# First group of a fused attention and two-layer expert kernel: float64 weights converted in double slabs on ScalarE and VectorE

## The chip, the cores and the metric

The kernel runs as one program on one core of a Trainium2 chip. The metric is the device time of one execution in microseconds; three runs of the kernel before took 1424.27, 1425.4 and 1425.7 us (median 1425.4).

## The reference

Three stages over 4608 tokens of width 512. Attention is within chunks of 64 tokens. The second stage's weights arrive as float64, everything else that is multiplied as float32.

```python
# q, k, v: 8 batches, 8 heads, 576 positions, 64 wide; chunks of 64
scores = scale * np.matmul(q_c, k_c.transpose(0, 1, 2, 4, 3))
attn = softmax(scores)
x = np.matmul(attn, v_c)              # to 4608 x 512, float32
h = x @ w_in                          # 512 x 2048, float64
g = h * (1.0 / (1.0 + np.exp(-h)))
x = (g @ w_out).astype(np.float32)    # 2048 x 512, float64
logits = x @ w_gate + modality_bias[modality_id]
e_idx = np.argmax(logits, axis=1)     # one of 8 experts per token
for e in range(8):                    # w1: 8 x 512 x 1024, w2: 8 x 1024 x 512
    h = np.maximum(x[e_idx == e] @ w1[e], 0.0)
    out[e_idx == e] = gate_w * (h @ w2[e])
```

## The kernel before

The tokens are worked in 18 blocks of 256 (two tiles of 128). A block goes through its attention, the first product with w_in (16 columns f of 128 hidden values), the activation, and the second product with w_out. Every value that enters a product of these two layers is cut in two parts, high and low, so that three products in a faster format stand for one in float32: `hi*x_hi`, `hi*x_lo`, `lo*x_hi` (L452, L483 to L485).

Blocks 0 and 1 form the **first group**: they run together, column by column, while w_in and w_out are still being read and converted. The converted weights then stay on chip (`big1`, `big2`) for the other 16 blocks, which run one at a time. A group has 18 steps: step st does the first product of column st and, two steps later (`LAG`), the second product of column st - 2. In the first group a step has two half steps, one for each block.

A **slab** is 128 columns of w_in or 128 rows of w_out, 512 KB of float64. Its conversion has four parts:

- `load_w64`: a DMA on SP's queue into one of four buffers, issued in the program's order when the slab four places earlier has been converted;
- `conv_p`: ScalarE takes the absolute value of the high words (L381), VectorE a maximum with a constant (L382);
- `conv_a`, all on VectorE: shift and mask (L395), the sign and top bit merged in (L399), the top bits of the low word merged in (L403); the result is float32;
- `conv_b`: ScalarE casts to the high part (L424), GpSimd subtracts to get the low part (L426).

One slab is converted in each half step, two half steps or more ahead of its use. The activation of a column is g = (tanh(h/2) + 1) h: tanh on ScalarE (L459, `th`), the rest on VectorE (L461, `g`). `g_parts` cuts it into `gh` on ScalarE (L467) and `gl`, on GpSimd in the first group (L470) and on VectorE later. The hidden values h stand in PSUM tiles `psh` of one bank each, of which there are two; a block's half step uses half of a bank.

Each engine runs its instructions in the order in which the program writes them; `weave` emits the parts of several generators in turn. Attention of the next block's tiles is spread over the half steps by lists (`att_side`). Before the first group stands the attention of tiles 0 to 3 in eight turns, with short products that nothing reads (`heat`) in between, and with the first slabs' conversion placed by `CONV_TURNS`. The queue of SP carries nearly all loads and stores, in order. When the conversion is done its memory becomes the pool `late`, which holds among others `wgb`, the router's weights, copied to all partitions; `dot` (L505) reads them on VectorE, a few per step (`pump`).

Of the kernel before, what the change touches and what calls it, by code (L numbers as in the profile page):

```python
# [42 lines left out]
def attention_moe_moe_kernel(  # L43
# [71 lines left out]
    def consts():  # L115
# [3 lines left out]
        # triu[r, c] = 1 where r < c  # L119
# [9 lines left out]
        # the tiles in the order of the experts, the lone one left out  # L129
# [224 lines left out]
    raw64 = {}  # L354
    # first layer's slabs, 2 f + (0: w_in, 1: w_out), in the order in which they are needed
    ORD = [0, 2] + [x for f in range(NF - 2) for x in (2 * f + 1, 2 * f + 4)] + [2 * NF - 3, 2 * NF - 1]
    w_in32 = w_in.bitcast(U32).rearrange("(k p) (f w) -> p k f w", p=P, w=2)
    w_out32 = w_out.bitcast(U32).rearrange("(f p) (d w) -> f p d w", p=P, w=2)

    def load_w64(conv, n):  # L360
        if n >= 2 * NF:
            return
        f, i = divmod(ORD[n], 2)
        if i == 0:
            a = conv.tile([P, KD, P, 2], U32, tag="raw", bufs=RAWB, name="ra")
# [976 lines left out]
```

## Time and profile before

| | us |
|---|---|
| runs, median of 3 | 1425.4 (1424.27 to 1425.7) |
| span of the profiled execution | 1423.4 |
| TensorE busy | 1385.9 (97%) |
| VectorE busy | 996.3 (70%) |
| ScalarE busy | 612.3 (43%) |
| GpSimd busy | 236.2 (17%) |

The profile is of one execution. Its span runs from the first to the last instruction; the runs' median is 2.0 us above it. The profiler's names for the engines are PE (TensorE, with PEld for its weight loads), DVE (VectorE), ACT (ScalarE), POOL (GpSimd) and SP (the queue that issues the DMAs). The duration of an instruction on VectorE or ScalarE holds some time in which the next one has already started, so that what a row of instructions costs is read from start to start.

### The profile page before, as it was taken

What the parts mean: (1) busy time and instruction counts of PE and PEld (TensorE: products, weight loads), DVE (VectorE), ACT (ScalarE), POOL (GpSimd) and SP (SyncE); (2) the same over time, 40 slices, a digit from 0 to 9 for tenths busy, and PEclk for the clock granted to TensorE, in tenths of its full rate; (3) what the DMA queues carried; (4) which work ended last, traced back from release to release, by engine and by line L of the source; (5) the groups of instructions that cost most, each with busy time, mean ns of one, the idle gap of its engine ahead of it and who ended that gap; (6) DMA issues with size and microseconds to landing.
All of it is one profiled execution on the core that took longest, in us unless ns stands there. A gap on an engine that the chain in (4) does not pass through costs nothing. (4 is left out here: it accounts for less than half of the span.)

```text
span 1423.4 us, 26828 instructions
## 1 busy us (share of the span) xinstructions
PE 1385.9 (97%) x9819; PEld 1231.9 (87%) x9819; DVE 996.3 (70%) x2430; ACT 612.3 (43%) x1294; POOL 236.2 (17%) x237
## 2 busy tenths in 40 slices
PE   8878999999999999999999999999999999999997
PEld 7767889888888888988888888889889998898996
DVE  6999678667766766766776677675577666666664
ACT  5454333333333333333333333343455555555554
POOL 2665300000000000000000000021322323232311
PEclk9899999999999999999999999999999999999999
DMA  8643413212311321321231132051677766676662
GB/s 202 169 125 116 144 35 61 52 30 40 60 30 32 60 42 20 60 52 29 40 60 29 32 60 38 12 130 39 205 249 217 235 217 222 207 233 212 221 219 85
DMA packets 246747, 153.82 MB, mean 108 GB/s; under 512 B 189730, under 2 KB 197958, under 8 KB 246480
## 3 DMA queue, kind: packets, MB, share of 16 engines
q1 hardware_dynamic: 238352, 133.07, 35.9%
q0 software_dynamic: 8256, 18.96, 3.7%
q8 instruction: 79, 1.29, 0.4%
q14 instruction: 60, 0.49, 0.1%
HBM read 132.48 MB, written 20.01 MB: 107 GB/s over the span
## 5 line engine op out<-in xcount | busy, mean ns | idle before, releaser
L452 PE MATMUL psh<-xh,big 128*128 128x256 f32 x2304 | 465.2, 287 | 18.4 <-DVE g L461 18.2
L452 PEld LDWEIGHTS psh<-xh,big 128*128 128x128 f32 x2304 | 376.0, 191 | 39.2 <-DVE g L461 26.0
L452 PE MATMUL psh<-xl,big 128*128 128x256 f32 x1152 | 326.3, 283 | 0.0
L452 PEld LDWEIGHTS psh<-xl,big 128*128 128x128 f32 x1152 | 219.5, 191 | 7.9 <-DVE xl L351 0.2
L461 DVE SCALAR_TENSOR_TENSOR g<-th,psh 128x256 f32<-128x256 f32 x288 | 120.2, 417 | 139.9 <-ACT th L459 138.9
L483 PE MATMUL psc<-big,gh 128*128 128x512 f32 x544 | 218.0, 401 | 0.0
L914 PE MATMUL psh<-xgh,big 128*128 128x256 f32 x1152 | 217.4, 281 | 0.2 <-DVE big L731 0.2
L485 PE MATMUL psc<-big,gl 128*128 128x512 f32 x544 | 214.7, 395 | 2.1 <-DVE gl L470 2.1
L484 PE MATMUL psc<-big,gh 128*128 128x512 f32 x544 | 215.5, 396 | 0.0
L459 ACT ACTIVATE th<-psh 128x256 f32<-128x256 f32 x288 | 110.3, 383 | 200.1 <-PE psh L452 195.9
L505 DVE CUSTOM_DVE_ANT_0 dump<-x2t,wgb 128x512 bf16<-128x512 f32 x272 | 185.0, 680 | 8.2 <-ACT x2t L494 6.4
L467 ACT CAST gh<-g 128x256 fp32r<-128x256 f32 x288 | 116.8, 405 | 166.4 <-DVE g L461 166.0
L914 PEld LDWEIGHTS psh<-xgh,big 128*128 128x128 f32 x1152 | 181.7, 188 | 3.7 <-DVE big L731 0.5
L602 POOL DMA_INDIRECT perm<-rpg,rdi x36 | 36.9, 1025 | 763.6 <-DVE rdi L601 634.8
L914 PE MATMUL psh<-xgl,big 128*128 128x256 f32 x576 | 161.9, 281 | 0.2 <-DVE xgl L905 0.2
L924 DVE SCALAR_TENSOR_TENSOR hl<-psh,hh 128x256 fp32r<-128x256 f32 x144 | 60.8, 424 | 126.1 <-ACT hh L923 126.1
L923 ACT ACTIVATE hh<-psh 128x256 fp32r<-128x256 f32 x144 | 55.4, 385 | 187.8 <-PE psh L914 185.7
L470 DVE TENSOR_TENSOR gl<-g,gh 128x256 fp32r<-128x256 f32 x256 | 107.6, 420 | 25.3 <-ACT gh L467 25.3
L485 PEld LDWEIGHTS psc<-big,gl 128*128 128x128 f32 x544 | 102.4, 188 | 26.2 <-DVE gl L470 2.6
L483 PEld LDWEIGHTS psc<-big,gh 128*128 128x128 f32 x544 | 103.0, 189 | 16.2 <-issue 2.7
L484 PEld LDWEIGHTS psc<-big,gh 128*128 128x128 f32 x544 | 102.6, 189 | 13.3
L914 PEld LDWEIGHTS psh<-xgl,big 128*128 128x128 f32 x576 | 108.8, 189 | 3.8 <-DVE xgl L905 0.5
(237 smaller groups left out, 2073.7 us busy)
## 6 DMA issues: line engine op xcount, KB each, us to landing
rb<-in_moe_w_dram SPq DMA_DIRECT2D x144, 256.0 KB
wr<-in_moe_w_dram SPq DMA_DIRECT2D x68, 512.0 KB
x2d<-x2t SPq DMA_DIRECT2D x36, 256.0 KB
ra<-in_moe_w_in_dram SPq DMA_DIRECT2D x16, 512.0 KB
rb<-in_moe_w_out_dram SPq DMA_DIRECT2D x16, 512.0 KB
qk<-in_q_dram SPq DMA_DIRECT2D x240, 32.0 KB
qk<-in_k_dram SPq DMA_DIRECT2D x240, 32.0 KB
vn<-in_v_dram SPq DMA_DIRECT2D x28, 256.0 KB
```

Source lines behind the costliest of these rows:

```text
L452: nc.tensor.matmul(hps[:, :256], lhsT=w, rhs=x[:, kk, :], start=n == 0, stop=n == 3 * KD - 1)
L459: nc.scalar.activation(out=th, in_=hps[:, :256], func=ACTF.Tanh, scale=0.5)
L461: nc.vector.scalar_tensor_tensor(out=g, in0=th, scalar=1.0, in1=hps[:, :256], op0=ALU.add, op1=ALU.mult)
L467: nc.scalar.copy(gh, g)
L470: eng.tensor_tensor(out=gl, in0=g, in1=gh.bitcast(F32), op=ALU.subtract)
L483: nc.tensor.matmul(a, lhsT=gh[:, c], rhs=wh, start=f == 0, stop=False)
L484: nc.tensor.matmul(a, lhsT=gh[:, c], rhs=wl, start=False, stop=False)
L485: nc.tensor.matmul(a, lhsT=gl[:, c], rhs=wh, start=False, stop=f == NF - 1)
L505: nc.vector.tensor_tensor_reduce(out=dump, in0=x2[j][t], in1=wg[0][:, e, :], scale=1.0, scalar=0.0, op0=ALU.mult, op1=ALU.add, accum_out=l ...
L914: nc.tensor.matmul(hp[:, :256], lhsT=w[:, part, :], rhs=x[:, :, kk * P:(kk + 1) * P], start=i == 0, stop=i == 3 * KD - 1,)
L923: nc.scalar.activation(out=gh, in_=hp[:, :256], func=ACTF.Relu)
L924: nc.vector.scalar_tensor_tensor(out=gl, in0=hp[:, :256], scalar=0.0, in1=gh.bitcast(F32), op0=ALU.max, op1=ALU.subtract)
```

## The change

Slabs become twice as large: 256 columns of w_in or 256 rows of w_out, 1 MB, 16 in all instead of 32, with two buffers instead of four. One double slab is converted per step. In place of absolute value and maximum ScalarE makes one scaled copy of the high words (times 2^-112); the shift's mask and the merge's mask are other constants, so that only the sign comes from the word itself. The subtraction for the low part goes from GpSimd to VectorE, and so does `gl` in the first group. Both blocks' first products of a column go into the two halves of one PSUM bank, and one tanh, one g, one gh and one gl of 512 serve both (`g_pair`). tanh is written in place of g everywhere, and gh and gl share one kind of buffer (`hid`, 5 of 512). At the start the first double slab is loaded behind tile 0's q and k, the second one between the values of tiles 1 and 2. The pool `late` is opened after the group's last step instead of after the last but one, and the dot products of the router start in the fifth step of the next group. (Comments were taken out as well.)

```diff
-RAWB = 4  # float64 slabs that are on chip at a time
+RAWB = 2
-CONV_TURNS = ((2, 2, 3, 6), (3, 3, 5), (4, 6))
+CONV_TURNS = ((1, 6), (1, 6), (2,))
...
+    DS = [(0, 0)] + [x for i in range(NF // 2 - 1) for x in ((0, i + 1), (1, i))] + [(1, NF // 2 - 1)]
+    w_in64 = w_in.bitcast(U32).rearrange("(k p) (i c) -> i p k c", p=P, c=4 * P)
+    w_out64 = w_out.bitcast(U32).rearrange("(i a p) c -> i p a c", p=P, a=2)
...
-        c = conv.tile([P, 512], U32, tag="cc", bufs=RAWB, name="cc")
-        nc.scalar.activation(out=c.bitcast(F32), in_=r3[:, :, 1].bitcast(F32), func=ACTF.Abs)
+        c = conv.tile([P, 1024], U32, tag="cc", bufs=2, name="cc")
+        nc.scalar.activation(
+            out=c.bitcast(F32), in_=raw64[n][:, :, 1].bitcast(F32), func=ACTF.Copy, scale=2.0 ** -112
+        )
...
+        x, r = c64.pop(n), raw64.pop(n)
         nc.vector.tensor_scalar(
-            out=c.bitcast(F32), in0=c.bitcast(F32), scalar1=2.0 ** -15, scalar2=None, op0=ALU.max
-        )
...
-            out=x, in0=c, scalar1=3, scalar2=0x3FFFFFF8, op0=ALU.logical_shift_left, op1=ALU.bitwise_and
+            out=x, in0=x, scalar1=3, scalar2=0x7FFFFFFF, op0=ALU.logical_shift_left, op1=ALU.bitwise_and
         )
         yield
         nc.vector.scalar_tensor_tensor(
-            out=x, in0=hw, scalar=0xC0000000, in1=x, op0=ALU.bitwise_and, op1=ALU.bitwise_or
+            out=x, in0=r[:, :, 1], scalar=0x80000000, in1=x, op0=ALU.bitwise_and, op1=ALU.bitwise_or
         )
         yield
         nc.vector.scalar_tensor_tensor(
-            out=x, in0=lw, scalar=29, in1=x, op0=ALU.logical_shift_right, op1=ALU.bitwise_or
+            out=x, in0=r[:, :, 0], scalar=29, in1=x, op0=ALU.logical_shift_right, op1=ALU.bitwise_or
         )
         y64[n] = x.bitcast(F32)
-        load_w64(conv, n + RAWB)
+        load_w64(n + RAWB)
...
         nc.scalar.copy(hi_o, y)
         yield
-        nc.gpsimd.tensor_tensor(out=lo_o, in0=y, in1=hi_o.bitcast(F32), op=ALU.subtract)
+        nc.vector.tensor_tensor(out=lo_o, in0=y, in1=hi_o.bitcast(F32), op=ALU.subtract)
...
+    def g_pair(f):
+
+        hps = gps.pop((0, f))
+        g = sb.tile([P, 512], F32, tag="g", bufs=3, name="gp")
+        nc.scalar.activation(out=g, in_=hps, func=ACTF.Tanh, scale=0.5)
+        nc.vector.scalar_tensor_tensor(out=g, in0=g, scalar=1.0, in1=hps, op0=ALU.add, op1=ALU.mult)
+        yield
+        gh = hid("gph", [P, 512])
+        nc.scalar.copy(gh, g)
+        yield
+        gl = hid("gpl", [P, 512])
+        nc.vector.tensor_tensor(out=gl, in0=g, in1=gh.bitcast(F32), op=ALU.subtract)
+        for n in range(2):
+            gst[n, f] = (gh[:, n * 256:(n + 1) * 256], gl[:, n * 256:(n + 1) * 256])
...
+        load_w64(0)
         load_nat(1, "qk")
...
-        for names, t in (("qk", 2), (None, 0), (None, 1), ("qk", 3), (None, 2), (None, 3), ("v", 0), ("v", 3),
-                         ("v", 2), ("v", 1)):
-            load_nat(t, names) if names else load_w64(conv, t)
+        for names, t in (("qk", 2), ("qk", 3), ("v", 0), ("v", 1), (None, 1), ("v", 2), ("v", 3)):
+            load_nat(t, names) if names else load_w64(t)
...
                 if first:
+                    hps = ps_h() if st < NF else None
                     for n, j in enumerate(blks):
...
-                        gens += [g_parts(j, st - 1, nc.gpsimd)] if 1 <= st <= NF else []
-                        gens += [once(conv_p, conv, hs + 4), conv_b(hs + 2), conv_a(conv, hs + 3)]
                         if n == 0:
...
+                            gens = [g_pair(st - 1)] if 1 <= st <= NF else []
+                            gens += [fn() for fn in side[2 * st]] + [conv_b(st + 1)]
+                        else:
+                            conv_p(st + 2)
+                            gens = [fn() for fn in side[2 * st + 1]] + [conv_a(st + 2)]
                         weave(gens)
                         if st < NF:
-                            g1_mm(j, st)
+                            g1_mm(j, st, hps[:, n * 256:(n + 1) * 256])
...
-                    gens += pump(2 if last or len(rq) > 16 else 1)
+                    if gi_ > 1 or st >= 4:
+                        gens += pump(2 if last or len(rq) > 16 else 1)
...
-                if first and st == nsteps - 2:
-                    conv_cm.__exit__(None, None, None)
...
             if first:
+                conv_cm.__exit__(None, None, None)
```

Three places in the order of the instructions follow. On VectorE, a half step of the first group before, with a w_out slab (`rb`; `cc` is the slab being converted, `psh` the hidden values):

```order
L461 SCALAR_TENSOR_TENSOR g<-th,psh 128x256
L382 TENSOR_SCALAR cc<-cc 128x512
L395 TENSOR_SCALAR cc<-cc 128x512
L399 SCALAR_TENSOR_TENSOR cc<-rb,cc 128x512
L403 SCALAR_TENSOR_TENSOR cc<-rb,cc 128x512
```

and a step of the first group now (`gp`, `gph` and `gpl` are g, gh and gl of both blocks, `big_70` the converted w_out, `ra` a w_in slab):

```order
L459 SCALAR_TENSOR_TENSOR gp<-gp,psh 128x512
L417 TENSOR_TENSOR big_70<-cc,big_70 128x1024
L465 TENSOR_TENSOR gpl<-gp,gph 128x512
L388 TENSOR_SCALAR cc<-cc 128x1024
L392 SCALAR_TENSOR_TENSOR cc<-ra,cc 128x1024
L396 SCALAR_TENSOR_TENSOR cc<-ra,cc 128x1024
```

Two half steps of five instructions became one step of six: the maximum is gone, the two subtractions L417 and L465 are new, and the rest has twice the elements. On ScalarE, the half step before in which tile 4's transposed q and k are copied (`qT`, `kT`; `big_69` is the converted w_in):

```order
L424 CAST big_69<-cc 128x4x128
L459 ACTIVATE th<-psh 128x256
L231 COPY qT<-psa 128x512
L231 COPY kT<-psa 128x512
L467 CAST gh<-g 128x256
L381 ACTIVATE cc<-rb 128x512
```

and the step now:

```order
L458 ACTIVATE gp<-psh 128x512
L231 COPY qT<-psa 128x512
L231 COPY kT<-psa 128x512
L415 CAST big_70<-cc 128x1024
L462 CAST gph<-gp 128x512
L378 ACTIVATE cc<-ra 128x1024
```

The slab's cast stood ahead of the copies and stands behind them now. On SP, the first DMAs before (`nat` is q, k or v of a tile):

```order
L178 DMA nat<-in_q_dram 128x8x64
L178 DMA nat<-in_k_dram 128x8x64
L178 DMA nat<-in_q_dram 128x8x64
L178 DMA nat<-in_k_dram 128x8x64
L178 DMA nat<-in_q_dram 128x8x64
L178 DMA nat<-in_k_dram 128x8x64
L366 DMA ra<-in_moe_w_in_dram 128x4x256 x2
```

and now:

```order
L178 DMA nat<-in_q_dram 128x8x64
L178 DMA nat<-in_k_dram 128x8x64
L367 DMA ra<-in_moe_w_in_dram 128x4x512
L178 DMA nat<-in_q_dram 128x8x64
L178 DMA nat<-in_k_dram 128x8x64
```

The first slab, which stood behind three tiles' q and k, stands behind those of tile 0.

## Rows read from the trace of the kernel before

**Rows 1.** The page: span, busy time, share and instructions of each engine.

```profile
span 1423.4 us, 26828 instructions
...
PE 1385.9 (97%) x9819; PEld 1231.9 (87%) x9819; DVE 996.3 (70%) x2430; ACT 612.3 (43%) x1294; POOL 236.2 (17%) x237
```

**Rows 2.** Busy time by stretch (us from the start), granted clock, DMA share, GB/s.

```profile
core 0: us, PE busy (x) PEld busy (x) DVE busy (x) ACT busy (x) POOL busy (x), PEclk, DMA share, GB/s
0.00:31.30 31.30, 28.16 (x488) 25.39 (x488) 19.32 (x42) 14.71 (x28) 4.51 (x24) 1.00 0.89 203
31.30:161.80 130.50, 109.53 (x737) 92.36 (x733) 117.02 (x169) 61.95 (x141) 78.44 (x66) 0.93 0.49 141
161.80:971.00 809.20, 806.79 (x5774) 716.86 (x5774) 580.79 (x1677) 298.68 (x698) 41.16 (x40) 1.00 0.24 47
```

**Rows 3.** Waits, 31.3 to 161.8 us: waiter, waited for, total, times, longest.

```profile
PE psh L452 <- DVE g L461: 17.9, 16, 2.2
```

**Rows 4.** Timeline of VectorE: start, duration, line, operation, operands.

```profile
47.72 0.41 DVE L461 SCALAR_TENSOR_TENSOR g<-th,psh 128x256 f32<-128x256 f32 x1
48.05 0.41 DVE L382 TENSOR_SCALAR cc<-cc 128x512 f32<-128x512 f32 x1
48.38 0.41 DVE L395 TENSOR_SCALAR cc<-cc 128x512 uint32<-128x512 uint32 x1
48.83 1.67 DVE L399 SCALAR_TENSOR_TENSOR cc<-ra,cc 128x512 uint32<-128x512 uint32 x1
50.53 1.12 DVE L403 SCALAR_TENSOR_TENSOR cc<-ra,cc 128x512 uint32<-128x512 uint32 x1
51.57 0.41 DVE L461 SCALAR_TENSOR_TENSOR g<-th,psh 128x256 f32<-128x256 f32 x1
```

**Rows 5.** Timeline of GpSimd at the same time.

```profile
48.53 1.42 POOL L426 TENSOR_TENSOR big<-cc,big 128x512 fp32r<-128x512 f32 x1 [1.28 <-ACT big L424]
```

**Rows 6.** Timeline of VectorE in the first attention, GpSimd idle.

```profile
20.07 1.28 DVE L399 SCALAR_TENSOR_TENSOR cc<-ra,cc 128x512 uint32<-128x512 uint32 x2
...
30.11 0.69 DVE L403 SCALAR_TENSOR_TENSOR cc<-rb,cc 128x512 uint32<-128x512 uint32 x1
```

**Rows 7.** Timeline of ScalarE, first attention and first group.

```profile
13.99 1.24 ACT L381 ACTIVATE cc<-ra 128x512 f32<-128x512 f32 x2
...
51.69 0.62 ACT L424 CAST big<-cc 128x512 fp32r<-128x512 f32 x1 [2.09 <-DVE cc L403]
...
52.49 0.58 ACT L231 COPY qT<-psa 128x512 f32<-128x512 f32 x1
...
53.43 0.43 ACT L467 CAST gh<-g 128x256 fp32r<-128x256 f32 x1
```

**Rows 8.** DMA, 80 to 100 us in 40 slices: GB/s moved.

```profile
GB/s 0 0 0 98 311 352 287 16 0 0 0 0 72 141 338 371 127 0 0 0 164 254 328 295 8 0 0 0 135 256 365 289 21 0 0 98 123 221 410 225
```

**Rows 9.** Timeline of TensorE in the first attention: transposes, scores, values of a tile.

```profile
8.90 1.10 PE L227 MATMUL psa<-ident,nat 128*128 128x128 f32 x8
...
10.73 1.15 PE L253 MATMUL psa<-kT,qT 64*64 64x64 f32 x32 [0.50 <-ACT kT L231]
...
26.02 0.97 PE L328 MATMUL psa<-pT,nat 64*64 64x64 f32 x32
```

**Rows 10.** Timeline of VectorE: the last step of tile 3's softmax.

```profile
27.78 0.69 DVE L274 TENSOR_TENSOR p<-p,sm 128x512 f32<-128x512 f32 x1
```

**Rows 11.** Timeline of TensorE at the first group's end, clock up.

```profile
153.24 0.28 PE L452 MATMUL psh<-xh,big 128*128 128x256 f32 x1
...
154.67 0.39 PE L483 MATMUL psa<-big,gh 128*128 128x512 f32 x1
...
156.06 0.40 PE L483 MATMUL psc<-big,gh 128*128 128x512 f32 x1
...
161.42 0.40 PE L485 MATMUL psa<-big,gl 128*128 128x512 f32 x1
```

**Rows 12.** Timeline of SP: issue of a DMA.

```profile
154.41 0.33 SPq L1158 DMA_DIRECT2D wgb<-wgt_d  x1
```

More of the change, by code (lines that the diff above doesn't have):

```diff
@@ L362, in load_w64 @@
+    w_in64 = w_in.bitcast(U32).rearrange("(k p) (i c) -> i p k c", p=P, c=4 * P)
+    w_out64 = w_out.bitcast(U32).rearrange("(i a p) c -> i p a c", p=P, a=2)
+    raw64, c64, y64 = {}, {}, {}
+    def load_w64(n):
+        if n >= NF:
             return
-        f, i = divmod(ORD[n], 2)
-        if i == 0:
-            a = conv.tile([P, KD, P, 2], U32, tag="raw", bufs=RAWB, name="ra")
-            nc.sync.dma_start(out=a, in_=w_in32[:, :, f * P:(f + 1) * P, :])
-        else:
-            a = conv.tile([P, 512, 2], U32, tag="raw", bufs=RAWB, name="rb")
-            nc.sync.dma_start(out=a, in_=w_out32[f])
@@ L387, in conv_a @@
-    def conv_a(conv, n):
-        if n >= 2 * NF:
-            return
-        del raw64[n]
-        c, r3 = c64.pop(n)
-        lw, hw = r3[:, :, 0], r3[:, :, 1]
-        x = c
-        nc.vector.tensor_scalar(
-            out=x, in0=c, scalar1=3, scalar2=0x3FFFFFF8, op0=ALU.logical_shift_left, op1=ALU.bitwise_and
+        which, i = DS[n]
+        if which == 0:
+            a = conv.tile([P, KD, 2 * P, 2], U32, tag="raw", bufs=RAWB, name="ra")
+            nc.sync.dma_start(out=a.rearrange("p k f w -> p k (f w)"), in_=w_in64[i])
+        else:
+            a = conv.tile([P, 2, 512, 2], U32, tag="raw", bufs=RAWB, name="rb")
+            nc.sync.dma_start(out=a.rearrange("p a d w -> p a (d w)"), in_=w_out64[i])
@@ L412, in conv_b @@
             return
[L413 to L414 removed]
         y = y64.pop(n)
[L416 to L418 removed]
+        which, i = DS[n]
+        half, fi = divmod(2 * i, 8)
+        if which == 0:
+            b = big1[:, half * 4:half * 4 + 4, :, fi * P:(fi + 2) * P]
+            hi_o, lo_o = b[:, :, 0], b[:, :, 1]
             y = y.rearrange("p (k f) -> p k f", k=KD)
         else:
[L421 to L423 removed]
+            hi_o, lo_o = big2[:, half * 4 + fi // 2, 0], big2[:, half * 4 + fi // 2, 1]
         nc.scalar.copy(hi_o, y)
         yield
[L426 removed]
+        nc.vector.tensor_tensor(out=lo_o, in0=y, in1=hi_o.bitcast(F32), op=ALU.subtract)
     def weave(gens):
@@ L441, in g1, with g1_mm @@
         g1_act(j, f)
-    def g1_mm(j, f):
+    def g1_mm(j, f, hps=None):
         half, fi = divmod(f, 8)
         hi, lo = xT[j]
-        hps = ps_h()
+        hps = ps_h() if hps is None else hps
         n = 0
@@ L920, in G1 @@
             del xgT[u]
-        gh = sb.tile([P, 256], F32R, tag="gh", bufs=5, name="hh")
-        gl = sb.tile([P, 256], F32R, tag="gl", bufs=5, name="hl")
+        gx = hid("h", [P, 2, 256])
+        gh, gl = gx[:, 0], gx[:, 1]
         nc.scalar.activation(out=gh, in_=hp[:, :256], func=ACTF.Relu)
@@ L996, in attention_moe_moe_kernel @@
         turns = [[] for _ in range(8)]
-        for part, at in zip((lambda n: once(conv_p, conv, n), lambda n: conv_a(conv, n), conv_b), CONV_TURNS):
+        for part, at in zip((lambda n: once(conv_p, n), conv_a, conv_b), CONV_TURNS):
             for n, i in enumerate(at):
@@ L1150, in attention_moe_moe_kernel @@
                     finish_step(j, st)
-                if first and st == nsteps - 2:
-                    conv_cm.__exit__(None, None, None)
-                    late_cm = tc.tile_pool(name="late", bufs=1)
-                    late = late_cm.__enter__()
-                    late_p.append(late)
-                    diag_open()
-                    wgb = late.tile([P, E, DM], F32, name="wgb")
-                    nc.sync.dma_start(
-                        out=wgb.rearrange("p e d -> p (e d)"),
-                        in_=wgt_d.rearrange("(o e) d -> o (e d)", o=1).to_broadcast([P, E * DM]),
-                    )
-                    wg.append(wgb)
-                if not first or st >= NF:
+                if not first:
                     late_gens = pump_late()
             if first:
+                conv_cm.__exit__(None, None, None)
+                late_cm = tc.tile_pool(name="late", bufs=1)
+                late = late_cm.__enter__()
+                late_p.append(late)
+                diag_open()
+                wgb = late.tile([P, E, DM], F32, name="wgb")
+                nc.sync.dma_start(
+                    out=wgb.rearrange("p e d -> p (e d)"),
+                    in_=wgt_d.rearrange("(o e) d -> o (e d)", o=1).to_broadcast([P, E * DM]),
+                )
+                wg.append(wgb)
                 router_bias()
```

61 lines of the change are left out of this document (22 added, 39 removed).

## The prediction

> **What bounds the kernel now.** I read the page's first part, then the busy time by stretch, then the waits of one stretch, then the timelines of single engines there. TensorE is busy in 97% of the span [rows 1], so only a stretch in which it is not can give time back. By stretch, the reader is to see that from 161.8 us on TensorE lacks 2.4 us in 809, while the first group (31.3 to 161.8 us, from its first product to the last of its second products) has it busy for 109.5 of 130.5 us, and at a mean granted clock of 0.93 instead of 1.00; VectorE is busy there for 117.0 us [rows 2]. The waits of that stretch put 17.9 us of TensorE's idle time down to VectorE's g [rows 3]. VectorE's own timeline shows why: a half step is five instructions, back to back, from 47.72 to 51.57, so 3.85 us, of which the two merges of the bits take 1.70 and 1.04 us from start to start [rows 4]. GpSimd works beside them, on its subtraction of one slab (1.42 us) and on gl [rows 5]. The stretch is bound by VectorE; what the change is worth is decided in it and at its two ends.
>
> **What a step costs on VectorE after the change.** First the prices without GpSimd beside. Where GpSimd is idle, two merges of 512 take 1.28 us together and one alone 0.69, so 0.60 from start to start [rows 6]; with g at 256 elements at 0.33 [rows 4] that is 0.27 per 256 elements and 0.06 fixed, hence 1.14 for 1024. The shift (0.33 for 512 [rows 4]) then takes 0.60 for 1024, and an instruction that needs the one ahead of it starts 0.12 later (0.45 against 0.33 behind L395). The max of L382 (32 x 0.33, so 10.6 us in all) goes. GpSimd's two subtractions come to VectorE.
>
> A step of both blocks was two half steps, 7.7 us. It becomes: g of both blocks 0.60, subtraction of a double slab 1.14, gl 0.60, shift 0.72, merges 1.26 and 1.14: 5.46 us. One wait is new: the subtraction needs the cast on ScalarE, which starts when the last merge ends. Casts of 256 and 512 took 0.43 and 0.62 [rows 7], so one of 1024 about 1.0; g covers 0.60 of it, and behind the drain of the merge (0.69 against 0.60) some 0.55 us remain open. Before, that subtraction stood on GpSimd and VectorE had no such wait. A step is then 6.0 us. The bounds: 5.5, if something hides the wait, and 6.9, if every cast and copy of ScalarE stands in the way. ScalarE itself has room: per step 0.6 + 1.0 + 0.6 for tanh, cast and gh, and 1.1 for the scaled copy (two of 512 took 1.24 [rows 7]), 3.3 of 6.0 us.
>
> The Trainium skill (Perfetto Trace Analysis, section Optimizing Scalar/DVE Operations) says that larger operations help a saturated engine, and that breaking instructions up lets others start sooner where the engine is not saturated. Both ends of it are at work here: by the first half alone, with nothing waiting, the step would be 5.46 us and the total some 7 us below my sum; the second half speaks against the change, and is the third rival's mechanism. The trace bears out the small fixed part (0.06 us); the wait it cannot show, since the cast's reader was GpSimd.
>
> **The start.** A load of 1 MB now goes between tile 0's k and tile 1's q. Half a megabyte moves in four slices of 0.5 us at up to 352 GB/s [rows 8], so 1 MB holds tile 1 up by 2.8 (at 371) to 5 us (at the 203 of the first 31.3 us [rows 2]); not all of that is lost, since its transposes at 8.90 [rows 9] stood behind the scores of tile 0. On the other side two slabs' merges between tiles 2 and 3 go, and one double slab comes between tiles 0 and 1. I take a loss of 2.5 us, between 0 and 5, until tile 3's softmax ends (27.78 + 0.61, so 28.4 before [rows 10]): 30.9. Behind it stand, in a row: its transposes 0.55, its values 0.97 [rows 9], copy 0.35, scaled copy 1.1, shift 0.72, a part of x 0.33, merges 1.26 and 1.14, two parts of x 0.67, cast 1.0, subtraction 1.14: 9.2 us. VectorE begins step 0's conversion at 40.1.
>
> **The sum of the first group.** From 40.1: step 0's conversion 3.1; thirteen steps of 6.0, 78.0; the softmax of tiles 4 and 5, four instructions of 0.60 and two small ones each, 2.7 x 2 = 5.4. That is 126.6, when the last conversion is done. Then g, gl and the last subtraction (3.3 with the cast's wait), and TensorE's second products of three columns of slabs, six times 1.39 [rows 11], 8.3, with some 0.4 between: 12.0. The group ends at 138.6 instead of 161.8: 23.2 us less. TensorE's own work does not forbid it: 32 x (1.43 + 1.39) = 90.2 [rows 11], two tiles of attention at 1.10 + 1.15 + 0.55 + 0.97 = 3.8 each [rows 9], about 1 for the router's tables: 98.8 us, from 33.8 on 132.6 us. At 5.64 a step against VectorE's 6.0 it can run about a step ahead, which is why tile copies on ScalarE should find their input ready.
>
> **The end of the group.** The router's table wgb (2 MB) was issued at 154.41, ahead of the x2 stores [rows 12]; now it is queued on SP behind tile 6's loads and four stores that wait for the end of the group. It lands perhaps 10 us behind the group's end (3 MB at some 350 GB/s [rows 8], and an estimated 1.5 us of issue and landing). Its reader, the dot product, now starts four steps into the next group, 2.9 + 2 x 2.8 = 8.5 us after the end, and TensorE goes on for another 4.2 us before it needs the gl queued behind that. I count 1 us for it, 0 to 3. All behind it runs at TensorE's pace [rows 2] and moves up as it is: in these blocks g, gh and gl keep their sizes, and the tanh written in place saves nothing that is waited for.
>
> The span is 1423.4 us, 2.0 below the runs' median of 1425.4, and I let those 2.0 stand: 1425.4 - 23.2 + 1 = 1403.
>
> **The rivals.**
> TensorE becomes the bound. If the cast's wait is hidden and the start is as good as before, the group ends at about 132.6 + 2 for the second block's first product, whose x stands behind the merges: 27 us less, 1398. For it: 5.46 is below 5.64. Against it: the cast starts only when the merge ends, and nothing stands between but g.
>
> ScalarE's order decides. It now has the copies of tiles 4 and 5 (0.58 each [rows 7]) between tanh and the cast. If TensorE is not a step ahead there, VectorE waits for transposes, copies and cast: 2.6 us at each of two transposes, 2.1 and 1.5 at tile 4's other two places, 9 us in all: 1412. Against it: TensorE's slack of 0.36 us a step. For it: the granted clock. Its mean in the stretch was 0.93, so part of it ran at 1.2 GHz rather than 2.4, after stretches in which TensorE waited for VectorE [rows 2, 3]; such a part would use up that slack.
>
> Slower: the loads decide. With two slab buffers, the load of a slab is issued when the merges of the slab two before it are done, so that two steps hold a load, a scaled copy (1.1) and a conversion (3.1) in a row. Two steps were 15.4 us: the point from which this loses is a landing of 11.2 us. At 13, seven rounds of 17.2 from 40.1 on and 12 behind them give 172.5, so 1436. Against it: half the size moved in 2 us [rows 8], and 1 MB should land in 5 and with tile 5's loads ahead of it in 8, of 8 that there are.
>
> It does not do what it says: the merges are slow (1.67 and 1.12) because they read every other word, not because of GpSimd. Then they cost 3.3 and 2.2 at 1024, a step 9.1, the group ends near 182, and the time is 1446. Against it: the same two instructions at 0.60 [rows 6]. The Trainium skill (SBUF — State Buffer, section Who interferes with whom) says that a VectorE instruction with two inputs in SBUF and a GpSimd one that reads SBUF exclude each other for a whole instruction. The trace agrees nearly: GpSimd's ran from 48.53 to 49.95, and the merge that started at 48.83 ended 0.55 us behind it [rows 4, 5].
>
> **How the numbers follow.** Forecast (1400 to 1408) 0.57; TensorE the bound (1395 to 1400) 0.17; ScalarE's order (1408 to 1417) 0.18; loads 0.03; slow merges 0.02; gains that cancel against a worse start 0.03. The range 1396 to 1413 leaves out the slow cases, the far end of the third and a little at the fast end. A difference of 0.2%, 2.9 us, is about what a measurement of this kernel can tell from none. Faster: 0.57 + 0.17 + 0.18 and part of the last, 0.93; same 0.02; slower 0.05.
>
> **What would show it.** Right: no GpSimd in the first group, merges of 1024 at 1.2 us, a step of 6.0 with one gap of about half a microsecond ahead of the subtraction, and TensorE's last second product near 139. The start is wrong if the first product comes outside 31 to 37. ScalarE's order shows as VectorE waiting over 1.5 us for a cast at the steps with transposes; late loads as the scaled copy waiting for a DMA; late wgb as VectorE waiting at the first dot product. Merges over 1.5 us with GpSimd idle would make the whole prediction wrong.

## The result, and the profile after

The changed kernel takes 1402.53 us (median of four runs, 1401.92 to 1404.24); the kernel before, run beside it, 1425.52 (1424.27 to 1425.7). The ratio is 0.9844, with an interval of 0.983 to 0.9858. The forecast was 1403.

The page of the changed kernel, first its span, then busy time, share and instructions of each engine:

```profile
span 1401.2 us, 26526 instructions
...
PE 1376.9 (98%) x9819; PEld 1228.8 (88%) x9819; DVE 969.0 (69%) x2366; ACT 605.8 (43%) x1230; POOL 160.6 (11%) x173
```

The span is 22.2 us shorter than [rows 1]. Its busy time by stretch, with the granted clock behind POOL's column, answers to [rows 2]:

```profile
core 0: us, PE busy (x) PEld busy (x) DVE busy (x) ACT busy (x) POOL busy (x), PEclk, DMA share, GB/s
36.00:144.10 108.10, 100.77 (x732) 89.22 (x732) 91.34 (x113) 55.23 (x80) 2.38 (x3) 0.98 0.55 156
144.10:951.00 806.90, 806.90 (x5782) 717.11 (x5782) 581.55 (x1678) 299.12 (x700) 41.67 (x40) 1.00 0.25 49
...
38.00:40.00 2.00, 0.00 (x0) 0.00 (x0) 1.97 (x4) 0.30 (x1) 0.00 (x0) 1.00 0.00 0
...
42.00:44.00 2.00, 2.00 (x11) 2.00 (x11) 1.93 (x4) 0.59 (x1) 0.00 (x0) 0.50 1.02 394
44.00:46.00 2.00, 2.00 (x14) 2.00 (x13) 1.72 (x2) 0.84 (x1) 0.00 (x0) 0.69 1.33 215
...
100.00:138.00 38.00, 38.00 (x267) 33.96 (x266) 32.06 (x41) 18.57 (x27) 1.85 (x2) 1.00 0.35 110
```

Three things are to be seen. In the first group TensorE now lacks 7.3 us instead of 21, and VectorE is no longer the busier engine there. From 100 us to the group's end TensorE is busy without a gap. And behind the group nothing at all is missing, where 2.4 us were before. TensorE's waits in the first group are others than [rows 3]; the 17.9 us for g are gone (xl is the low part of x, the first product's input; qT and p belong to the attention of tiles 4 and 5):

```profile
PE psh L443 <- DVE xl L351: 2.7, 1, 2.7
PE psa L253 <- DVE xl L351: 2.1, 1, 2.1
PE psa L636 <- ACT qT L231: 1.8, 1, 1.8
PE psa L283 <- DVE p L274: 0.6, 1, 0.6
```

VectorE's timeline over one plain step (start, duration, line, operation, operands) answers to [rows 4]:

```profile
47.98 0.69 DVE L388 TENSOR_SCALAR cc<-cc 128x1024 uint32<-128x1024 uint32 x1
48.70 1.22 DVE L392 SCALAR_TENSOR_TENSOR cc<-ra,cc 128x1024 uint32<-128x1024 uint32 x1
49.96 1.23 DVE L396 SCALAR_TENSOR_TENSOR cc<-ra,cc 128x1024 uint32<-128x1024 uint32 x1
51.11 0.68 DVE L459 SCALAR_TENSOR_TENSOR gp<-gp,psh 128x512 f32<-128x512 f32 x1
52.30 1.23 DVE L417 TENSOR_TENSOR big<-cc,big 128x1024 fp32r<-128x1024 f32 x1 [0.52 <-ACT big L415]
53.44 0.68 DVE L465 TENSOR_TENSOR gpl<-gp,gph 128x512 fp32r<-128x512 f32 x1
54.05 0.69 DVE L388 TENSOR_SCALAR cc<-cc 128x1024 uint32<-128x1024 uint32 x1
...
127.44 1.23 DVE L396 SCALAR_TENSOR_TENSOR cc<-rb,cc 128x1024 uint32<-128x1024 uint32 x1
```

A step is 6.07 us, the merges 1.22, the one wait 0.52 us.

**Where the 22.2 us are.** Block 1's result leaves PSUM when the first group ends, block 17's when the first layer ends. ScalarE's timeline of these copies (start, duration of a block's two together) in the kernel before:

```profile
161.16 1.30 ACT L494 ACTIVATE x2t<-psa 128x512 f32<-128x512 f32 x2
...
972.83 1.30 ACT L494 ACTIVATE x2t<-psc 128x512 f32<-128x512 f32 x2 [1.89 <-PE psc L485]
```

and in the changed one:

```profile
143.52 1.30 ACT L502 ACTIVATE x2t<-psa 128x512 f32<-128x512 f32 x2
...
950.79 1.30 ACT L502 ACTIVATE x2t<-psc 128x512 f32<-128x512 f32 x2 [1.90 <-PE psc L493]
```

The first group gave 17.6 us (161.16 to 143.52). The stretch from there to block 17 shrank from 811.7 to 807.3 us: 4.4 more, where I had expected none. The last 0.2 lie behind it. So the total was forecast to half a microsecond, and its two parts were each off by over 5 us.

The place of the 4.4 us is the last block. In the kernel before GpSimd writes block 15's token lists, which say what token goes to which expert (L602), and reads the first expert's (L875), and VectorE waits for what was read. The timelines of the three engines, with the wait in brackets:

```profile
927.10 1.17 POOL L602 DMA_INDIRECT perm<-rpg,rdi  x1 [4.15 <-DVE lg L505]
935.01 1.40 POOL L875 DMA_INDIRECT idg<-perm,gidx  x1 [6.74 <-DVE lg L505]
...
942.45 0.15 DVE L882 CAST oi<-idg 128x1 uint32<-128x1 f32 x1 [1.92 <-DMA idg<-perm,gidx]
...
944.34 0.50 PE L485 MATMUL psc<-big,gl 128*128 128x512 f32 x1 [2.14 <-DVE gl L470]
```

and the granted clock behind that, in the same kernel:

```profile
946.00:948.00 2.00, 2.00 (x10) 1.98 (x10) 1.52 (x5) 0.93 (x2) 0.00 (x0) 0.50 0.37 126
```

From the last writing to the first reading 7.9 us pass. VectorE stands in four waits (4.9 us in all), gl is queued behind them, TensorE stands 2.14 us, and its granted clock falls to 0.50, the lower of its two levels. In the changed kernel the two issues are 6.2 us apart and TensorE does not stand:

```profile
908.54 1.30 POOL L610 DMA_INDIRECT perm<-rpg,rdi  x1 [3.67 <-DVE lg L513]
914.72 1.18 POOL L883 DMA_INDIRECT idg<-perm,gidx  x1 [4.87 <-DVE lg L513]
```

### The profile page after: what moved, and what is told of

Same layout as the page of the kernel before. It is cut to its first block, busy times and chain, and to the rows that moved or that the text cites. A ratio compares the mean times of both kernels' runs of the same rounds, so it can differ in the third digit from the quotient of the medians.

```text
span 1401.2 us, 26526 instructions
## 1 busy us (share of the span) xinstructions
PE 1376.9 (98%) x9819; PEld 1228.8 (88%) x9819; DVE 969.0 (69%) x2366; ACT 605.8 (43%) x1230; POOL 160.6 (11%) x173
## 5 line engine op out<-in xcount | busy, mean ns | idle before, releaser
L443 PE MATMUL psh<-xh,big 128*128 128x256 f32 x2304 | 456.9, 284 | 0.1
L443 PEld LDWEIGHTS psh<-xh,big 128*128 128x128 f32 x2304 | 371.8, 189 | 14.3 <-issue 4.5
L491 PE MATMUL psc<-big,g 128*128 128x512 f32 x512 | 204.8, 400 | 0.0
L492 PE MATMUL psc<-big,g 128*128 128x512 f32 x512 | 202.4, 395 | 0.0
L493 PE MATMUL psc<-big,g 128*128 128x512 f32 x512 | 201.8, 394 | 0.0
L451 DVE SCALAR_TENSOR_TENSOR g<-g,psh 128x256 f32<-128x256 f32 x256 | 107.2, 419 | 132.2 <-ACT g L450 130.9
L450 ACT ACTIVATE g<-psh 128x256 f32<-128x256 f32 x256 | 98.1, 383 | 196.0 <-PE psh L443 188.4
L476 ACT CAST g<-g 128x256 fp32r<-128x256 f32 x256 | 103.9, 406 | 163.3 <-DVE g L451 159.2
L932 DVE SCALAR_TENSOR_TENSOR h<-psh,h 128x256 fp32r<-128x256 f32 x144 | 60.7, 424 | 127.2 <-ACT h L931 124.2
L931 ACT ACTIVATE h<-psh 128x256 fp32r<-128x256 f32 x144 | 55.3, 385 | 188.9 <-PE psh L922 159.0
L478 DVE TENSOR_TENSOR g<-g 128x256 fp32r<-128x256 f32 x256 | 107.6, 420 | 24.9 <-ACT g L476 24.9
L493 PEld LDWEIGHTS psc<-big,g 128*128 128x128 f32 x512 | 96.1, 188 | 22.1
L491 PEld LDWEIGHTS psc<-big,g 128*128 128x128 f32 x512 | 96.5, 188 | 15.4 <-issue 2.7
L492 PEld LDWEIGHTS psc<-big,g 128*128 128x128 f32 x512 | 96.2, 188 | 12.4
```

The costliest lines, as they stand in the source:

```text
L443: nc.tensor.matmul(hps[:, :256], lhsT=w, rhs=x[:, kk, :], start=n == 0, stop=n == 3 * KD - 1)
L450: nc.scalar.activation(out=g, in_=hps[:, :256], func=ACTF.Tanh, scale=0.5)
L451: nc.vector.scalar_tensor_tensor(out=g, in0=g, scalar=1.0, in1=hps[:, :256], op0=ALU.add, op1=ALU.mult)
L476: nc.scalar.copy(gh, g)
L478: nc.vector.tensor_tensor(out=gl, in0=g, in1=gh.bitcast(F32), op=ALU.subtract)
L491: nc.tensor.matmul(a, lhsT=gh[:, c], rhs=wh, start=f == 0, stop=False)
```

## The experiments

Each ratio is to the kernel before, run on the same chip beside it; that took 1425.5 us beside the changed kernel, 1423.6 beside runs 1 to 4 and 9 to 12, and 1424.0 beside runs 5 to 8, so that runs of different rows are compared by their ratios. From the traces: the start of the first group's first product, the start of block 1's copy out of PSUM, the time between them, and the time from there to block 17's copy.

| run | median us | ratio [interval] | first product | block 1 out | between | to block 17 |
|---|---|---|---|---|---|---|
| before | 1425.5 | 1 | 31.3 | 161.2 | 129.8 | 811.7 |
| changed | 1402.5 | 0.9844 [0.983, 0.9858] | 35.9 | 143.5 | 107.6 | 807.3 |
| 1 | 1420.3 | 0.998 [0.9969, 0.9992] | 35.0 | 155.0 | 120.1 | 812.1 |
| 2 | 1408.2 | 0.9892 [0.9878, 0.9906] | 31.8 | 147.5 | 115.7 | 809.7 |
| 3 | 1399.9 | 0.9831 [0.9818, 0.9843] | 30.2 | 138.0 | 107.8 | 811.7 |
| 4 | 1420.1 | 0.9977 [0.9968, 0.9986] | 31.3 | 161.2 | 129.9 | 807.7 |
| 5 | 1402.0 | 0.9847 [0.9834, 0.986] | 34.4 | 141.4 | 107.1 | 807.5 |
| 6 | 1401.4 | 0.9839 [0.9825, 0.9852] | 34.5 | 142.9 | 108.5 | 808.0 |
| 7 | 1405.1 | 0.9873 [0.9858, 0.9889] | 36.0 | 144.6 | 108.6 | 807.7 |
| 8 | 1395.9 | 0.9802 [0.9789, 0.9816] | 30.0 | 137.6 | 107.6 | 807.7 |
| 9 | 1403.0 | 0.9861 [0.9846, 0.9876] | 35.3 | 144.4 | 109.1 | 807.3 |
| 10 | 1420.0 | 0.9978 [0.9969, 0.9987] | 31.2 | 161.1 | 129.9 | 807.7 |
| 11 | 1399.8 | 0.9836 [0.9823, 0.985] | 36.2 | 141.7 | 105.5 | 807.3 |
| 12 | 1398.0 | 0.9825 [0.9812, 0.9839] | 34.1 | 139.8 | 105.8 | 807.8 |

Run 9's first group is that of the changed kernel: its 109.1 us against 107.6 says what one profile can differ by.

### Which part pays: runs 1 to 3

**Run 1**, GpSimd back in:

```diff
-        nc.vector.tensor_tensor(out=lo_o, in0=y, in1=hi_o.bitcast(F32), op=ALU.subtract)
+        nc.gpsimd.tensor_tensor(out=lo_o, in0=y, in1=hi_o.bitcast(F32), op=ALU.subtract)
```

> The changed kernel with only the slab's subtraction (1024 wide, lo_o) put back on GpSimd. Theory A (a GpSimd operation and a VectorE operation with two SBUF inputs keep each other out): GpSimd needs about 2 x 1.42 = 2.8 us for it, the VectorE work with two SBUF inputs in a step is two merges and gl, 1.26 + 1.14 + 0.60 = 3.0 us, so a step is 5.8 us or a little more, and in the trace the merges beside GpSimd's subtraction take 2 us or more instead of 1.22; the time stays within 3 us of the changed kernel's, 1400 to 1408, though VectorE has 1.14 us of work and 0.5 us of waiting less in each step. Theory B (GpSimd's work is free beside VectorE, merges stay at 1.22): the step falls to 4.4 us on VectorE, TensorE is the bound, and the time falls 3 us or more below the changed kernel's, to 1399 or less.

It took 1420.3 us, far outside theory A's range of 1400 to 1408: nearly the whole gain is gone, 12.5 us of it in the first group and 4.8 behind it (see the transition, below), although VectorE has 1.14 us of work and a wait less in each step. VectorE's and GpSimd's timelines of this run:

```profile
61.42 2.46 DVE L465 TENSOR_TENSOR gpl<-gp,gph 128x512 fp32r<-128x512 f32 x1 [1.03 <-ACT gph L462]
...
64.52 1.23 DVE L392 SCALAR_TENSOR_TENSOR cc<-ra,cc 128x1024 uint32<-128x1024 uint32 x1
```

```profile
60.95 2.39 POOL L417 TENSOR_TENSOR big<-cc,big 128x1024 fp32r<-128x1024 f32 x1 [4.84 <-ACT big L415]
```

The instruction that GpSimd holds up is here gl: 2.46 us for one that takes 0.68 alone, ending 0.54 us behind GpSimd's (60.95 + 2.39 = 63.34). The merges, no longer beside GpSimd, stay at 1.23. A step is 7.2 us. Theory A has the mechanism, and its size for a step, 5.8, was too small: I had counted only busy times, not gl's new wait for gh (1.03 us) ahead of the lock. Theory B is out.

**Run 2**, the kernel before with GpSimd out of the first group and nothing else:

```diff
-        nc.gpsimd.tensor_tensor(out=lo_o, in0=y, in1=hi_o.bitcast(F32), op=ALU.subtract)
+        nc.vector.tensor_tensor(out=lo_o, in0=y, in1=hi_o.bitcast(F32), op=ALU.subtract)
...
-                        gens += [g_parts(j, st - 1, nc.gpsimd)] if 1 <= st <= NF else []
+                        gens += [g_parts(j, st - 1, nc.vector)] if 1 <= st <= NF else []
```

> The kernel before, single slabs and single blocks, with only GpSimd's two operations of the first group moved to VectorE. Theory A (taking GpSimd away is what pays): merges of 512 fall from 1.67 and 1.10 to 0.69; a half step on VectorE is g 0.33, max 0.33, shift 0.33, subtraction 0.60, gl 0.33 and two merges 1.29, so 3.2 to 3.4 us instead of 3.85; 27 half steps give 12 to 17 us: 1409 to 1414. Theory B (larger and fewer instructions are what pays): VectorE has two instructions more per half step, the time stays within 3 us of 1425 or gets worse.

1408.2 us, 15.4 less than the kernel before beside it; block 1 leaves PSUM 13.7 us earlier. VectorE does two instructions more per half step and needs 3.27 us for it instead of 3.85, for the merges take 0.68 or 0.69 (VectorE's timeline):

```profile
61.10 0.68 DVE L399 SCALAR_TENSOR_TENSOR cc<-ra,cc 128x512 uint32<-128x512 uint32 x1
```

**Run 3**, the maximum gone too:

```diff
-        nc.scalar.activation(out=c.bitcast(F32), in_=r3[:, :, 1].bitcast(F32), func=ACTF.Abs)
-        nc.vector.tensor_scalar(
-            out=c.bitcast(F32), in0=c.bitcast(F32), scalar1=2.0 ** -15, scalar2=None, op0=ALU.max
+        nc.scalar.activation(
+            out=c.bitcast(F32), in_=r3[:, :, 1].bitcast(F32), func=ACTF.Copy, scale=2.0 ** -112
...
-            out=x, in0=c, scalar1=3, scalar2=0x3FFFFFF8, op0=ALU.logical_shift_left, op1=ALU.bitwise_and
+            out=x, in0=c, scalar1=3, scalar2=0x7FFFFFFF, op0=ALU.logical_shift_left, op1=ALU.bitwise_and
...
-            out=x, in0=hw, scalar=0xC0000000, in1=x, op0=ALU.bitwise_and, op1=ALU.bitwise_or
+            out=x, in0=hw, scalar=0x80000000, in1=x, op0=ALU.bitwise_and, op1=ALU.bitwise_or
```

> As the run before it (single slabs, GpSimd's two operations on VectorE), and the maximum on VectorE gone as in the change: one scaled copy on ScalarE in place of the absolute value, the other masks. Theory A: a further 0.33 us per half step off VectorE, now 2.9 to 3.1 us, close to TensorE's 2.82: 4 to 9 us more, so 1402 to 1408, about what the whole change reaches. Then double slabs and one bank for both blocks give nothing by themselves: what they save in fixed parts (0.06 us for each of six instructions a half step) they lose to the cast's wait. Theory B: the doubling carries a good part of the gain, and this run stays above 1410.

1399.9 us, better than expected: another 9.5 us in the first group, against 10.6 worked out for the maximum. With single slabs, and without the shared bank, the group takes 107.8 us from its first product, the changed kernel's 107.6. VectorE's two half steps take 5.86 us here, a double slab's step 6.07, and TensorE is busy for 100.8 us of the group in both. Doubling therefore shortens nothing once the group runs. But the changed kernel's group starts 5.7 us later (35.9 against 30.2) and ends 5.5 later. So in the first group taking GpSimd away gave 13.7, the maximum 9.5, and all else that the change does took 5.5 back. In the total less of that shows, since run 3 keeps the last block's stall (811.7); the two ratios' intervals overlap.

### The last block: runs 4, 9 and 10

**Runs 4 and 9** have the same edit, in the kernel before and in the changed one:

```diff
-                    side[12].append(lambda i=i: once(make_oid, i))
-                side[14].append(lambda: once(gather, 0))
-                side[14].append(lambda: once(gather, 1))
+                    side[16].append(lambda i=i: once(make_oid, i))
+                side[17].append(lambda: once(gather, 0))
+                side[17].append(lambda: once(gather, 1))
```

> The kernel before, with the last block's reading of the token lists (VectorE's four oi, and the two gathers behind them) four and three half steps later, so that VectorE reaches oi when the lists have landed. In the profile of the kernel before VectorE waits 4.9 us there and TensorE stands 2.1 us, then runs at 1.2 GHz for a while; in the profile of the changed kernel it does not. If that stall is in every run of the kernel before: 3 to 4.5 us less, 1421 to 1422.5, and block 17 takes 46 to 47 us instead of 50. If it is peculiar to the one execution that was profiled: within 1 us of 1425.

> The changed kernel with the same late edit that gave 3.5 us in the kernel before: the last block's reading of the token lists four half steps later. In the profile of the changed kernel VectorE waits 1.8 us there instead of 4.9 and TensorE does not stand at all. If some 4 us of the change's 23 came from that place (the change happens to take the stall away): within 1 us of the changed kernel, 1402 to 1403. If the stall is still there in most runs: 1398.5 to 1400.

Before: 1420.1, so 3.3 us less by the ratio and 4.0 in the profile, all of it behind block 1. Changed: 1403.0, nothing won (the ratios' intervals overlap), and the same 807.3 us. So the stall is in the timed runs of the kernel before, not just in the profiled one, and the change had taken it away without an edit at that place.

**Run 10** leaves that place alone and delays the first expert's loads instead. The choice of the expert loses its last two instructions to a function of its own, which is queued behind four dot products:

```diff
+    def choose_rows():
+        V = nc.vector
         V.scalar_tensor_tensor(
             out=gi, in0=gf.to_broadcast([P, 4]), scalar=4.0, in1=iota4, op0=ALU.mult, op1=ALU.add
         )
...
                 rq.append(("d", lambda i=i: once(dot, j, i)))
+                if j == NB - 2 and i == 3:
+                    rq.append(("d", lambda: once(choose_rows)))
```

> The kernel before; only the two instructions on VectorE that give the first expert's rows (gi and gidx0) are taken from the end of the choice to behind four dot products of the next block, so that the first expert's eight loads of 256 KB are issued some 3 to 5 us later, behind the two scatters into perm instead of beside them. Theory L (the scatter of the token lists lands late, 7.9 us, because four loads of 256 KB were issued ahead of it): it lands in 4 to 6 us, the reading of the lists comes earlier, VectorE's wait of 4.9 us shrinks to 2 or less, and the time falls by 2 to 4 us, 1420 to 1422. Rival (the scatter is slow by itself): no change, within 1 us of the kernel before.

1420.0 us, as theory L said. GpSimd's timeline of this run:

```profile
927.09 1.13 POOL L602 DMA_INDIRECT perm<-rpg,rdi  x1 [4.19 <-DVE lg L505]
933.33 0.98 POOL L876 DMA_INDIRECT idg<-perm,gidx  x1 [5.11 <-DVE gl L470]
```

With the first of the eight loads at 928.59 the lists are read 6.2 us after they are written, a little above what theory L expected, and VectorE's waits shrink to 2.14 us. The kernel before had issued four loads ahead of that writing at 927.10, the changed kernel two, ahead of 908.54. SP's timelines of the two:

```profile
925.22 0.36 SPq L698 DMA_DIRECT2D ra<-in_moe_w_dram  x1
...
927.02 0.33 SPq L701 DMA_DIRECT2D rb<-in_moe_w_dram  x1
```

```profile
908.09 0.35 SPq L709 DMA_DIRECT2D rb<-in_moe_w_dram  x1
908.70 1.58 SPq L706 DMA_DIRECT2D ra<-in_moe_w_dram  x1
```

What held the third one for 1.58 us in the changed kernel was not followed further. So run 10 shows that the loads make the stall in the kernel before; that the change took it away in the same manner is read from these rows and was not tested.

### What sets the end of the first group: runs 5, 6, 7, 11 and 12

**Run 5** hides the cast's wait:

```diff
-        nc.scalar.copy(hi_o, y)
+        if which:
+            hs = [(hi_o[:, c], lo_o[:, c], y[:, c]) for c in (slice(0, 512), slice(512, 1024))]
+        else:
+            hs = [(hi_o[:, c], lo_o[:, c], y[:, c]) for c in (slice(0, 2), slice(2, 4))]
+        for h, lw, r in hs:
+            nc.scalar.copy(h, r)
         yield
-        nc.vector.tensor_tensor(out=lo_o, in0=y, in1=hi_o.bitcast(F32), op=ALU.subtract)
+        for h, lw, r in hs:
+            nc.vector.tensor_tensor(out=lw, in0=r, in1=h.bitcast(F32), op=ALU.subtract)
```

> The changed kernel, with the cast to the high part and the subtraction behind it each cut in two halves of 512, so that the first half's cast (about 0.6 us) is hidden behind g (0.60). Nothing else. VectorE's step should fall from 6.06 to 5.6 or 5.7 us, since the wait of 0.52 us goes and one fixed part of 0.06 comes. Theory V (VectorE's step still sets the end of the first group, as my forecast had it): 13 steps of 0.4 us, so 4 to 5 us less than the changed kernel, 1397 to 1399. Theory T (TensorE, which is busy without a gap from 100 us on, sets it, and VectorE's wait costs nothing): within 1.5 us of the changed kernel, 1401 to 1403.

1402.0 us, which would speak for theory T, but the run does not tell the two apart, since the step hardly became shorter. VectorE's timeline, and ScalarE's behind it:

```profile
46.38 0.70 DVE L388 TENSOR_SCALAR cc<-cc 128x1024 uint32<-128x1024 uint32 x1 [0.20 <-ACT cc L378]
...
52.39 0.69 DVE L388 TENSOR_SCALAR cc<-cc 128x1024 uint32<-128x1024 uint32 x1 [0.21 <-ACT cc L378]
```

```profile
49.63 1.14 ACT L420 CAST big<-cc 128x512 fp32r<-128x512 f32 x2 [2.80 <-DVE cc L396]
50.68 0.61 ACT L468 CAST gph<-gp 128x512 fp32r<-128x512 f32 x1
51.20 1.16 ACT L378 ACTIVATE cc<-rb 128x1024 f32<-128x1024 f32 x1
```

The subtraction no longer waits, and the next shift does, for the scaled copy, which stands behind the casts and gh on ScalarE. The step is 6.01 us. A second chain, merge, cast, gh, scaled copy, shift, lay just under the first.

**Run 6**, the idle products ahead of tile 2's second transposes:

```diff
-HEAT = ((0, 20, 0), (0, 4, 0), (0, 10, 0), (8, 16, 0), (20, 0, 20), (44, 0, 0), (8, 0, 0), (0, 4, 0))
+HEAT = ((0, 20, 0), (0, 4, 0), (0, 10, 0), (8, 16, 0), (20, 0, 0), (0, 0, 0), (8, 0, 0), (0, 4, 0))
```

> The changed kernel without the 64 products that nothing reads which stand ahead of tile 2's second transposes (20 in turn 4, 44 in turn 5). In the trace they run from 27.8 to 31.5 us while tile 2's probabilities are ready at 27.5. Theory H (they are what makes the start late): everything behind them comes 2 to 3.5 us earlier, the first product at 32.5 to 34, VectorE's first conversion at about 39.5, and the time is 1399 to 1400.5. Rival (they are needed, or something else is late next): without them TensorE's granted clock falls to the lower of its two levels for the transposes, values and first products, or VectorE's softmax is late anyway, and the time stays within 1.5 us of the changed kernel's 1402.5 or goes above it.

In the changed kernel TensorE's timeline had them right in the way:

```profile
27.76 3.75 PE L1014 MATMUL psh<-ones 128*128 128x128 bf16 x64
...
35.92 0.39 PE L443 MATMUL psh<-xh,big 128*128 128x256 f32 x1
40.38 0.38 PE L443 MATMUL psh<-xl,big 128*128 128x256 f32 x1 [2.65 <-DVE xl L351]
```

Without them the first product starts at 34.5, and step 0's conversion 1.5 us earlier (40.45 instead of 41.92); the clock stayed at 1.00 up to 38 us and fell behind the wait for x, as in the changed kernel. Of the 1.5 us 0.6 is left at the group's end; the rest comes back as new waits of TensorE for gp (0.8 us). 1401.4 us is in the rival's range, by its second reason (something else is late next), and the interval does not part it from the changed kernel.

**Run 7** takes the two merges out of the way of x:

```diff
-CONV_TURNS = ((1, 6), (1, 6), (2,))
+CONV_TURNS = ((1, 6), (1, 7), (2,))
```

> The changed kernel, with the second double slab's shift and merges one turn later in the first attention (turn 7 instead of 6), so that the low parts of x of tiles 2 and 3 don't stand behind two merges of 1.2 us on VectorE. Nothing is taken away; VectorE's chain to the first subtraction keeps its length. Theory T (TensorE sets the end): its idle 2.65 us at 37.6 to 40.4 and the half clock behind it (about 1.6 us) go, and the time falls by 2 to 4 us, to 1398.5 to 1400.5. Theory V (VectorE's chain sets it): within 1 us of 1402.5.

1405.1 us: both theories missed. TensorE's wait for x shrank from 2.65 to 0.52 us, and a longer one came behind it, because the first subtraction on VectorE was now a microsecond later (41.79 instead of 40.78) and g of the first column stands behind that and the next conversion. TensorE's timeline, and two stretches with the granted clock:

```profile
46.79 0.58 PE L443 MATMUL psh<-xh,big 128*128 128x256 f32 x1 [4.03 <-DVE gp L459]
```

```profile
46.00:48.00 2.00, 1.21 (x5) 1.21 (x6) 1.49 (x3) 1.83 (x3) 0.00 (x0) 0.50 1.41 174
48.00:50.00 2.00, 2.00 (x12) 2.00 (x11) 1.97 (x4) 1.30 (x2) 0.00 (x0) 0.50 1.39 196
```

In this run, then, VectorE's chain sets TensorE's pace up to 46.8 us. In the changed kernel TensorE has no wait for gp there.

**Run 11** moves stages of tiles 4 and 5:

```diff
-                att_side(side, 4, (6, 9, 11, 14, 18), False)
-                att_side(side, 5, (16, 19, 21, 25, 28))
-                side[16].append(lambda: once(router_gate))
+                att_side(side, 4, (6, 9, 11, 15, 17), False)
+                att_side(side, 5, (16, 19, 21, 25, 29))
+                side[12].append(lambda: once(router_gate))
```

> The changed kernel with four stages of tiles 4 and 5 and the router's table at other half steps: second transposes of tile 4 from 14 to 15, its values from 18 to 17 (an odd half step, where ScalarE's copies don't stand behind a cast that waits for VectorE), tile 5's values from 28 to 29, the router's transposes from 16 to 12, away from tile 5's. No work is added or taken away. In the changed kernel's profile TensorE stands 0.6, 1.8 and 2.1 us at these three places. Theory T (TensorE sets the end of the group): 2.5 to 4 us less, 1398.5 to 1400. Theory V (VectorE's step does): within 1 us.

1399.8 us. VectorE's work and its step (6.06 us) are the same; the group is 105.5 us long, 2.1 and 3.6 us shorter than in the two executions of the unchanged one. Of TensorE's waits the three at the tiles (4.5 us) became two:

```profile
PE psh L443 <- DVE xl L351: 2.7, 1, 2.7
PE psa L227 <- ACT pT L285: 1.8, 1, 1.8
PE psh L443 <- DVE gp L459: 1.2, 1, 1.2
```

They are 1.5 us shorter together, and from 100 to 138 us TensorE again has no gap. In the profiles, then, TensorE's idle time in the middle of the group sets its end, as theory T says; a shorter VectorE step was not there to be tested. By the ratio alone the two kernels are not parted.

**Run 12** has the edits of runs 5, 6 and 11 together.

> The changed kernel with three edits together: cast and subtraction in halves, the 64 idle products ahead of tile 2's second transposes gone, and the stages of tiles 4 and 5 moved as in the run before. By theory T the first two gave 0.5 and 1.1 us alone because each engine held the other; together the group should end when TensorE's 98.8 us of work, the 2.65 us wait for the second block's x and 1.6 us of half clock have passed since a first product at 34.4: 137.5 instead of 144.1, so 1395.5 to 1397.5. Rival (each is worth what it is alone): 1.6 us and what the moved stages give, 1397 to 1400.

1398.0 us, in the rival's range. The group ends 3.7 us earlier than the changed kernel's, of which 1.8 are its start. TensorE now waits 2.2 us for gp and 1.9 for pT: with each wait removed the next one is closer. Most of the other 1.8 us is not the edits' doing in this execution: the clock did not fall behind the 2.67 us wait for x, where the fall cost the changed kernel about 1.6 us. The busy time of that stretch in this run, with the granted clock behind POOL's column:

```profile
36.00:56.00 20.00, 16.48 (x115) 15.14 (x115) 18.15 (x24) 10.24 (x16) 0.00 (x0) 1.00 0.78 198
```

The ratio's interval overlaps the changed kernel's.

### A version that beats both: run 8

The edits of runs 2, 3 and 4 together, in the kernel before.

> The kernel before with three edits: GpSimd's two operations of the first group on VectorE, the scaled copy in place of absolute value and maximum, and the last block's reading of the token lists four half steps later. Single slabs, single blocks. The first two gave 1399.9, the third 3.5 us by itself in the kernel before, and the profile of the first two still has block 17 at 50.8 us. If they add: 1396 to 1397, below both kernels. If the late stall has another cause there: 1399 to 1400.

1395.9 us, and the parts add. Its interval (0.9789 to 0.9816) lies wholly under the changed kernel's.

## Why the prediction was right, and where not

- **Prices.** Merges of 1024 at 1.26 and 1.15 from start to start (forecast 1.26 and 1.14), shift 0.72, a cast's wait of 0.52 (0.55), a step of 6.07 (6.0). The rival that the merges are slow by themselves is out; runs 1 and 2 show the cause. The loads are out too: ScalarE never stands idle ahead of a scaled copy in the first group.
- **The start.** Tile 3's softmax ended at 30.9, as forecast, and VectorE began step 0's conversion at 41.9 instead of 40.1. The step that failed is the row of instructions behind that softmax: I had not put TensorE's 64 idle products into it. Before they ran from 21.8 on, hidden; moving the work behind them made them late. Run 6 shows 1.5 us of it. The first product is 4.6 us later than before. Which part of that the 1 MB load has was not tried.
- **Thirteen steps and two tiles.** 41.9 to the last merge's end at 128.6 are 86.7 us, forecast 86.5.
- **The tail.** Forecast 12.0 behind the last conversion, measured 15.5 (to 144.1). This is the term that was mis-sized most. The sign I had named, TensorE's last second product near 139, did not come. I took it that TensorE's 98.8 us of work "does not forbid" VectorE's end. The 98.8 were right: 100.77 busy, less 1.6 for the half clock (1.0 at 42 to 44, 0.6 at 44 to 46). But from a first product at 35.9 they need, with 7.2 us of waits and 1.6 of half clock, until 143.5. TensorE was the bound of the group's second half, the first rival's mechanism, from a later start; and its waits at tiles 4 and 5 are those that the second rival looked for on VectorE, whose longest wait for a cast is 0.52. Run 11's profile shows that they count.
- **The transition.** wgb came 2.46 us late for VectorE at 155.05 and cost TensorE nothing; I had 1 us. In run 1 VectorE waited 7.25 us for it and TensorE then 2.7, with a lower clock behind (0.50 from 174 to 176 us): most of the 4.8 us by which that run's last column is longer than the changed kernel's.
- **Behind it.** That all behind the group "moves up as it is" was wrong by 4.4 us, a stall that the trace of before showed and that I had put among TensorE's 2.4 missing microseconds as if it were fixed. The half clock behind it, in which TensorE counts as busy, I did not add.

So -17.6 and -4.4 stand where I had -23.2 and +1. The mechanism on VectorE was right; that the time was right to half a microsecond is luck, for two errors of some 5 us had opposite signs.

## What to carry to other kernels

Look first for GpSimd beside VectorE instructions that read two SBUF operands: here moving GpSimd's work onto the busier engine made that engine faster. Try the parts of a compound change one at a time, since the doubling that looked like its core gave nothing once the group ran, and the start that came with it cost 5.5 us. When an engine's step shrinks to nearly that of the next engine, the sum has to be made for both, with each one's waits and half clock.

## What the runs showed of the hardware

- Which VectorE instruction pays for GpSimd is a matter of order: with slabs of 512 it was the merges (1.67 us), in run 1 gl (2.46), whichever of those with two inputs in SBUF started while GpSimd's ran. The Trainium skill (SBUF — State Buffer, section Who interferes with whom) says that the order of issue decides who blocks. Run 1 agrees: GpSimd's began 0.47 us ahead of gl, and gl ended 0.54 us behind it.
- From GpSimd's writing of rows of 8 bytes to their reading 6.2 us passed with no load of 256 KB issued ahead (run 10), 6.2 and 6.8 with two (the changed kernel, run 11), 7.5 to 8.5 with four (before, runs 2, 4 and 8). With three it was anything from 6.0 (run 9) to 8.6 (run 3), so the count is not all. In run 10 the 1.7 us less there came with 3.1 us less in total, by the ratio.
- Behind some of TensorE's stands its granted clock fell to 0.50: in the changed kernel at 42 to 44, after 2.65 us; in the kernel before at 946 to 948, after 2.14; in run 7 from 46 us on, at the end of 4.03. Behind others as long it stayed at 1.00: in run 12 after 2.67 us, and in the changed kernel after the 2.10 us that ended at 97.65. In these traces the length of a stand alone does not tell which it will be.

```profile
98.00:100.00 2.00, 2.00 (x38) 1.93 (x35) 2.00 (x4) 0.46 (x1) 0.00 (x0) 1.00 0.80 326
```

This row is the changed kernel's, right behind the stand of 2.10 us.
